# Thirty-two-byte gaps between the weight blocks of a fused attention and feed-forward kernel

## The chip, the core and the metric

The kernel runs on one core of a Trainium2 chip. The time is device microseconds of one execution, and the figure for a kernel is the median of several executions. Before the change the median of 3 runs is 677.4 us (677.21 to 677.68).

## The reference

Sliding-window attention with a few sink positions feeds a two-layer network whose first layer is followed by a leaky rectifier with one slope per hidden unit. All is float32.

```python
batch, n_heads, seq, head_dim = (4, 8, 768, 64); n_sink, window = (4, 128)
n_tokens, d_model, d_ff = (3072, 512, 2048)

scores = q @ k.T / 8;  keep = (pos_k < n_sink) | ((rel >= 0) & (rel < window))
a = exp(scores - max) / (sum + 1e-9);  attn = a @ v          # masked scores are -1e9
x = attn laid out as (3072, 512)
h = x @ w_in
g = maximum(h, 0) + alpha * minimum(h, 0)
return g @ w_out
```

## The kernel before

**Tiling.** The 3072 tokens are handled in 12 chunks of 256. In each chunk the attention of 8 heads is worked out, and its result stands in SBUF, transposed, as two tiles of four 128x256 blocks: `xh`, the value rounded to TensorE's fast float32 form, and `xl`, the rest. The hidden width of 2048 is cut into 16 blocks of 128, `f` = 0 to 15. A block's two weight matrices are in SBUF for the whole program in one tile `w0` to `w15` of 8192 bytes per partition: first `w_in`'s slice, high part and low part (2048 bytes each), then `w_out`'s slice, high and low part.

**The two products.** For each chunk and block, `gemm1` issues 12 matmuls (line 894): four steps along d_model, in each of them high weights by `xh`, high weights by `xl`, low weights by `xh`. The weights are the stationary operand (128 columns, 512 bytes per partition), `x` is the moving one (256 columns, 1024 bytes). The result is turned into `g` by lines 898 (ScalarE) and 899 (VectorE) and split into `gh` (line 900, ScalarE) and `gl` (line 901, VectorE). `gemm2` then issues 6 matmuls: here half of `gh` or `gl` is stationary (512 bytes) and a `w_out` slice moves (512 columns, 2048 bytes): lines 931 (high) and 932 (low) for each half of `gh`, and line 929 for each half of `gl`. Between a block's `gemm1` and its `gemm2` stand the products of the two blocks after it, and the attention of the next chunk is strewn between them. In all there are 12 x 16 x 12 = 2304 matmuls of the first and 12 x 16 x 6 = 1152 of the second kind, and each has a weight load of its own.

**The order.** A planner written in Python simulates the engines with a table of costs and fixes the order of all instructions on every engine while the program is built. It knows nothing of where in SBUF a tile lies. Around the place that the prediction reads, TensorE's order is (bank, moving or stationary tiles, shape):

```order
L894 MATMUL bank5_69<-xh1_116,w15_1207 128x256
L931 MATMUL bank6_70<-w13_1071,gh2_123 128x512
L932 MATMUL bank6_70<-w13_1071,gh2_123 128x512
L931 MATMUL bank7_71<-w13_1071,gh2_123 128x512
L932 MATMUL bank7_71<-w13_1071,gh2_123 128x512
L929 MATMUL bank6_70<-w13_1071,gl2_126 128x512
L929 MATMUL bank7_71<-w13_1071,gl2_126 128x512
L894 MATMUL bank4_68<-xh0_115,w0_305 128x256
...
L931 MATMUL bank6_70<-w14_1148,gh0_121 128x512
L932 MATMUL bank6_70<-w14_1148,gh0_121 128x512
```

So the second product of block 13 is followed by the first product of block 0 of the next chunk, and that by the second product of block 14.

**Where tiles lie.** Tiles are taken from pools. The pool `const` comes first in SBUF, and its tiles lie one behind the other in the order in which they are first asked for; each starts at a multiple of 32 bytes. A weight block's place is first asked for where its raw values are loaded (`load_weights`, line 371), the raw 64-bit values and the finished block share the tag `w{f}` and so the place. The places of blocks 13, 14 and 15 are first lent to tiles of the beginning (`lend`, lines 414 to 430). Behind `const` stands the pool `main` with `kq`, `pt_`, `comb`, `x`, `g` and the others.

Of the kernel before, what the change touches and what calls it, by code (L numbers as in the profile page):

```python
# [9 lines left out]
F32 = mybir.dt.float32  # L10
# [9 lines left out]
P = 128  # L20
# [58 lines left out]
class Plan:  # L79
# [20 lines left out]
    def held(self, tile_):  # L100
        v = Value(None)
        v.at = tile_
        return v

    def op(self, engine, cost, run, reads=(), writes=(), tail=0.09, mode=None, nbytes=0, other=None, locks=False):
        o = Op(engine, cost, tail, run, self.rank if engine == "PE" else None)
        o.ways = {engine: (cost, run)}
        if other:
            o.ways[other[0]] = other[1:]
        o.born = self.rank  # L110
        if engine == "PE":
            self.rank += 1
        o.mode, o.nbytes, o.index = mode, nbytes, len(self.ops)
        seen = []
        for group, writing in ((reads, False), (writes, True)):
            for x in group:
                v, key = x if isinstance(x, tuple) else (x, None)
                if v not in seen:
                    seen.append(v)
                keys = [k for k in set(v.wrote) | set(v.read) if key is None or k is None or k == key]  # L120
                for k in keys:
                    o.before.update(v.wrote.get(k, ()))
                    if writing:
                        o.before.update(v.read.get(k, ()))
                if writing:
                    for k in keys:
                        if key is None or k == key:
                            v.wrote.pop(k, None)
                            v.read.pop(k, None)
                    v.wrote.setdefault(key, []).append(o)  # L130
                else:
                    v.read.setdefault(key, []).append(o)
        for v in seen:
            v.left += 1
        o.values = seen
        o.takes = [v for v in seen if v.kind]
        o.locks = locks
        self.ops.append(o)
        return o
# [182 lines left out]
def program(ctx, tc, qk, pairs, vp, vq, vs, w, par, out):  # L322
    nc = tc.nc
    const = ctx.enter_context(tc.tile_pool(name="const", bufs=1))
# [42 lines left out]
    def load_weights(f, engine="ACT"):  # L367
        raw = raws[f] = held(None)

        def run():  # L370
            raw.at = const.tile([P, 2 * DM, 2], I32, tag=f"w{f}", name="wraw")
            (nc.sync if engine == "SP" else nc.scalar).dma_start(
                raw.at.rearrange("p (i x) w -> p i (x w)", i=2), w[f].bitcast(I32).rearrange("i p x -> p i x"))
        return op(engine, ISSUE if engine == "SP" else 0.12, run, writes=[raw] + lent.get(f, []), nbytes=8 * P * 2 * DM)
# [35 lines left out]
    lent = {}  # L410

    def lend(f, shape, count):
        box = {}

        def part(i):
            if "tile" not in box:
                box["tile"] = const.tile([P, count, *shape], F32, tag=f"w{f}", name="lent")
            return box["tile"][:, i]
        out_ = []
        for i in range(count):  # L420
            v = held(None)
            v.bind, v.box = lambda i=i: part(i), box
            out_.append(v)
        lent[f] = out_
        return out_

    early = lend(NF - 1, [QC + KC], 3) + lend(NF - 2, [QC + KC], 1)
    shared = const.tile([P, 1, QC + KC + 4 * WIN], F32, tag=f"w{NF - 2}", name="lent")
    early[3].box["tile"] = shared[:, :, :QC + KC]
    early_v = lend(NF - 3, [3, 2, D], 4)  # L430

    def bound(v):
# [845 lines left out]
```

## Time and profile before

| | before |
|---|---|
| median of 3 runs | 677.4 us |
| profiled execution, first to last instruction | 676.2 us |
| TensorE (PE) busy | 663.8 us, 98% of the span |
| weight loads (PEld) busy | 580.5 us, 86% |
| VectorE (DVE) busy | 525.8 us, 78% |
| ScalarE (ACT) busy | 397.5 us, 59% |
| granted TensorE clock, mean | 0.994 |

The span is the time from the first to the last instruction of one profiled execution; 1.2 us of the median lie around it. Matmuls are pipelined: a record's length runs from its start to the modelled end of its last column, and the next one starts long before that. What a matmul takes of TensorE's time is therefore read from the distance between the starts of two of them, not from the length of one.

### The profile page before, as it was taken

Reading aid. Unit: us, or ns where it says so; the run is one execution under the profiler, and the core shown is the slowest. Engines: PE = TensorE matmul, PEld = TensorE weight load, DVE = VectorE, ACT = ScalarE, POOL = GpSimd, SP = SyncE. Lnnn points to the kernel's source line nnn. Section 1 sums busy time; section 2 is a strip of 40 time slices with the busy share of each in tenths; the row PEclk is TensorE's granted clock in tenths of the full one; section 3 lists DMA queues with packets and bytes.
Section 4 is the critical chain, followed back from the end, with each engine's and each line's share of the span. In section 5 each row is a group of like instructions: output and inputs, shape, how many; then the busy total and the mean of one; then the engine's idle time right before and its main releaser. Section 6 shows DMA issues by size and latency. Waiting matters only on the chain.

```text
span 676.2 us, 13243 instructions
## 1 busy us (share of the span) xinstructions
PE 663.8 (98%) x4532; PEld 580.5 (86%) x4534; DVE 525.8 (78%) x1750; ACT 397.5 (59%) x1066; POOL 34.5 (5%) x115
## 2 busy tenths in 40 slices
PE   9989999999999999999999999999999999999996
PEld 4577898888989989989988988988998988998995
DVE  6999999968967976986986995995895994994331
ACT  6989888827636726736636735644744753853332
POOL 2110000001000000000000000010000000000000
PEclk9979999999999999999999999999999999999999
DMA  8684641424343453443443433552542543420001
GB/s 314 229 277 151 241 187 39 127 71 147 122 133 107 122 148 93 145 132 95 141 118 114 143 107 93 163 140 61 172 128 78 161 128 88 142 94 17 32 2 35
DMA packets 58683, 85.19 MB, mean 126 GB/s; under 512 B 9072, under 2 KB 35056, under 8 KB 58608
## 3 DMA queue, kind: packets, MB, share of 16 engines
q1 hardware_dynamic: 55056, 71.17, 34.7%
q10 hardware_dynamic: 3552, 13.11, 5.4%
q8 instruction: 37, 0.61, 0.4%
q14 instruction: 38, 0.31, 0.1%
HBM read 67.22 MB, written 17.04 MB: 125 GB/s over the span
## 4 chain that ended last, share of the span: by engine, by line
PE 83%; DVE 9%; ACT 5%; issue 2%; POOL 0%; DMA 0%; ACTq 0%; SPq 0%; POOLq 0%
PE bank L894 35%; PE bank L931 12%; PE bank L932 11%; PE bank L929 11%; PE bank L786 3%; PE bank L598 3%; PE bank L597 3%; PE bank L875 2%; DVE wa L396 2%; ACT pt L614 1%; ACT wa L382 1%; DVE wa L394 1%; DVE w L404 1%; DVE g L899 1%; DVE gl L901 1%
## 5 line engine op out<-in xcount | busy, mean ns | idle before, releaser
L894 PE MATMUL bank<-xh,w 128*128 128x256 f32 x1536 | 307.9, 283 | 0.4 <-DVE g L899 0.2
L894 PEld LDWEIGHTS bank<-xh,w 128*128 128x128 f32 x1536 | 250.6, 189 | 9.0 <-DVE g L899 3.0
L894 PE MATMUL bank<-xl,w 128*128 128x256 f32 x768 | 215.1, 280 | 0.1
L898 ACT ACTIVATE g<-bank,param 128x256 f32<-128x256 f32 x192 | 90.5, 472 | 117.4 <-PE bank L894 113.1
L931 PE MATMUL bank<-w,gh 128*128 128x512 f32 x382 | 151.7, 397 | 0.2 <-ACT gh L900 0.2
L932 PE MATMUL bank<-w,gh 128*128 128x512 f32 x382 | 150.1, 393 | 0.0
L894 PEld LDWEIGHTS bank<-xl,w 128*128 128x128 f32 x768 | 145.2, 189 | 4.4 <-DVE xl L808 0.3
L614 ACT ACTIVATE pt<-pt,nm 128x260 f32<-128x260 f32 (+1 forms) x192 | 94.5, 493 | 53.5 <-DVE nm L610 53.1
L899 DVE TENSOR_TENSOR g<-bank,g 128x256 f32<-128x256 f32 x192 | 79.7, 419 | 51.4 <-ACT g L898 50.9
L929 PE MATMUL bank<-w,gl 128*128 128x512 f32 x382 | 119.5, 394 | 0.0
L900 ACT CAST gh<-g 128x256 fp32r<-128x256 f32 x192 | 76.9, 404 | 59.7 <-DVE g L899 59.6
L901 DVE TENSOR_TENSOR gl<-g,gh 128x256 fp32r<-128x256 f32 x192 | 80.5, 423 | 26.5 <-ACT gh L900 23.0
L610 DVE CUSTOM_DVE_ANT_0 pt<-bank,masks 128x260 f32<-128x260 f32 (+1 forms) x192 | 75.0, 401 | 19.3 <-PE bank L598 15.5
L929 PEld LDWEIGHTS bank<-w,gl 128*128 128x128 f32 x382 | 70.7, 188 | 16.2 <-issue 0.7
L931 PEld LDWEIGHTS bank<-w,gh 128*128 128x128 f32 x382 | 71.9, 188 | 9.5 <-ACT gh L900 0.7
L932 PEld LDWEIGHTS bank<-w,gh 128*128 128x128 f32 x382 | 71.9, 188 | 8.3
L563 DVE TENSOR_TENSOR kq<-stage,kq 64x392 fp32r<-64x392 f32 x80 | 45.3, 566 | 2.7
L659 POOL TENSOR_TENSOR sink<-pt,ri 128x8 f32<-128x8 f32 x80 | 20.8, 264 | 504.7 <-DVE ri L644 358.8
L597 PE MATMUL bank<-kq 128*128 128x260 f32 (+1 forms) x160 | 44.4, 278 | 1.3 <-DVE nm L610 1.3
L598 PE MATMUL bank<-kq 128*128 128x260 f32 (+1 forms) x160 | 45.0, 281 | 0.0
L655 DVE CUSTOM_DVE_ANT_0 comb<-pt,ri 128x128 f32<-128x128 f32 x136 | 43.1, 343 | 0.4
L561 ACT CAST kq<-stage 128x392 fp32r<-128x392 f32 x80 | 40.9, 512 | 0.7 <-ACT pt L614 0.2
(130 smaller groups left out, 686.9 us busy)
## 6 DMA issues: line engine op xcount, KB each, us to landing
stage<-qk SPq DMA_DIRECT2D x80, 324.0 KB, 2.9
wraw<-w ACTq DMA_DIRECT2D x12, 1024.0 KB, 5.9
swap<-comb SPq DMA_DIRECT2D x36, 256.0 KB, 2.0
comb<-swap SPq DMA_DIRECT2D x36, 256.0 KB, 3.2
v<-vq SPq DMA_DIRECT2D x36, 192.0 KB, 2.5
out_dram<-ob SPq DMA_DIRECT2D x22, 256.0 KB, 3.5
wraw<-w SPq DMA_DIRECT2D x4, 1024.0 KB, 12.0
v<-vp SPq DMA_DIRECT2D x8, 192.0 KB, 6.9
```

Of the source, the lines that this page charges most:

```text
L597: nc.tensor.matmul(s[:, w0], qh()[:, qs], ks()[:, kw], start=True, stop=False)
L598: nc.tensor.matmul(s[:, w0], ql()[:, qs], ks()[:, kw], start=False, stop=True)
L610: op("DVE", dve(n), lambda: nc.vector.tensor_tensor_reduce(out=pt.at[:, u, w0], in0=s.at[:, w0], in1=masks[:, i, w0], scale=-0.125, scalar ...
L614: op("ACT", exp(n), lambda: nc.scalar.activation(pt.at[:, u, w0], pt.at[:, u, w0], AF.Exp, bias=nm.at[:, h, u:u + 1], scale=-1.0, accum_ou ...
L894: nc.tensor.matmul(h(), fin.at[:, 0, part, ks], rhs.at[:, kt], start=(kt == 0 and n == 0), stop=(kt == KT - 1 and n == 2))
L898: op("ACT", act(QC, True), lambda: nc.scalar.activation(g.at, h(), AF.Copy, scale=alt[:, f:f + 1]), reads=[bk, known("param")], writes=[g])
L899: op("DVE", dve(QC), lambda: nc.vector.tensor_tensor(g.at, h(), g.at, ALU.max), reads=[bk], writes=[g])
L900: op("ACT", cast(QC), lambda: nc.scalar.copy(gh.at, g.at), reads=[g], writes=[gh])
L901: op("DVE", dve(QC), lambda: nc.vector.tensor_tensor(gl.at, g.at, gh.at.bitcast(F32), ALU.subtract), reads=[g, gh], writes=[gl])
L929: nc.tensor.matmul(o2[j].at, gl.at[:, js], fin.at[:, 1, 0], start=False, stop=(f == NF - 1))
L931: nc.tensor.matmul(o2[j].at, gh.at[:, js], fin.at[:, 1, 0], start=(f == 0), stop=False)
L932: nc.tensor.matmul(o2[j].at, gh.at[:, js], fin.at[:, 1, 1], start=False, stop=False)
```

## The change

A tile of 8 floats (32 bytes per partition) is asked for ahead of each weight block whose place isn't lent, and one more behind the place that block 14 shares with the tiles of the beginning. Nothing reads or writes these tiles. No operation, no operand's shape, no order and no semaphore is another: on every engine the instructions stand in the same order as before, with the same waits.

```diff
@@ load_weights
         def run():
+            if f not in lent:
+                const.tile([P, 8], F32, name=f"gap{f}")
             raw.at = const.tile([P, 2 * DM, 2], I32, tag=f"w{f}", name="wraw")
@@ after lend(...)
     early[3].box["tile"] = shared[:, :, :QC + KC]
+    const.tile([P, 8], F32, name="gap")
     early_v = lend(NF - 3, [3, 2, D], 4)
```

What is another is where tiles start. In bytes modulo 512, by the program's own table of tiles:

| tile | before | after |
|---|---|---|
| w14 | 192 | 192 |
| w15 | 32 | 64 |
| w0, w13 | 32 | 96 |
| w1, w2, w3, ... w12 | 32 | 128, 160, 192, ... 480 (32 more each time) |
| xh, xl, g, gh, gl, sinkT, vs, ob (all) | 224 | 160 |
| comb, wa (all) | 256 | 192 |
| kq0, kq1 | 96, 128 | 32, 64 |
| ident | 320 | 352 |

A weight slice is 512 or a multiple of 512 bytes away from its block's start, and so is each part of `xh`, `xl`, `gh` and `gl`. So one number modulo 512 says where the two operands of all matmuls of a block lie to each other. For `gemm1` (place of `x` less place of the block) it was 192 for 15 blocks and 32 for block 14. It is now 64 for blocks 0 and 13, 32, 0, -32, -64, ... -320 for blocks 1 to 12 (-320 is 192 again), -32 for block 14 and 96 for block 15. For `gemm2` it is the same number with the other sign. Within the pool `main` all tiles are moved by the same 448 bytes.

## The prediction

> **What bounds the kernel now.** I looked first at the busy time by stretch, since no instruction is added or moved and only an engine that sets the end can pass a change on. Columns: stretch; its length; busy time and instructions of TensorE, of weight loads, VectorE, ScalarE and GpSimd; granted clock, DMA share, GB/s.
>
> ```profile
> 0.00:20.00 20.00, 18.34 (x98) 8.87 (x99) 13.47 (x61) 13.09 (x36) 4.40 (x22) 1.00 0.90 327
> 20.00:60.00 40.00, 37.13 (x235) 27.33 (x235) 38.16 (x86) 36.89 (x93) 5.24 (x10) 0.91 0.62 216
> 100.00:150.00 50.00, 49.42 (x333) 43.46 (x332) 44.81 (x149) 33.55 (x89) 2.72 (x8) 1.00 0.27 78
> 200.00:300.00 100.00, 100.00 (x689) 90.55 (x687) 82.31 (x303) 57.38 (x165) 5.28 (x17) 1.00 0.41 120
> 300.00:400.00 100.00, 100.00 (x699) 89.84 (x699) 79.54 (x293) 57.46 (x166) 3.99 (x16) 1.00 0.42 123
> 400.00:500.00 100.00, 100.00 (x711) 90.20 (x710) 78.75 (x285) 57.19 (x165) 5.36 (x17) 1.00 0.42 122
> ```
>
> From 200 us on TensorE never stops, at the full clock; before that it stops for 1 to 7% of a stretch. The other engines have room. So nearly every nanosecond that a matmul's start-to-start distance gains or loses goes into the time. Most of these matmuls are of the two products; the groups (busy time, mean length of one, idle time before) are:
>
> ```profile
> L894 PE MATMUL bank<-xh,w 128*128 128x256 f32 x1536 | 307.9, 283 | 0.4 <-DVE g L899 0.2
> L931 PE MATMUL bank<-w,gh 128*128 128x512 f32 x382 | 151.7, 397 | 0.2 <-ACT gh L900 0.2
> L932 PE MATMUL bank<-w,gh 128*128 128x512 f32 x382 | 150.1, 393 | 0.0
> L894 PE MATMUL bank<-xl,w 128*128 128x256 f32 x768 | 215.1, 280 | 0.1
> L929 PE MATMUL bank<-w,gl 128*128 128x512 f32 x382 | 119.5, 394 | 0.0
> ```
>
> They wait for almost nothing (0.2 us and less). What is left is how fast one matmul follows the other, and here the timeline has something odd. Four pieces of it follow, of TensorE alone (start, length, line, tiles): block 9's first product in one chunk and in the next, the second product of block 13, and that of block 14.
>
> ```profile
> 336.98 0.28 PE L894 MATMUL bank<-xl,w 128*128 128x256 f32 x1
> ...
> 338.28 0.28 PE L597 MATMUL bank<-kq 128*128 128x260 f32 x1
> ...
> 388.76 0.28 PE L894 MATMUL bank<-xl,w 128*128 128x256 f32 x1
> ...
> 390.01 0.28 PE L597 MATMUL bank<-kq 128*128 128x260 f32 x1
> 390.24 0.40 PE L931 MATMUL bank<-w,gh 128*128 128x512 f32 x1
> ...
> 391.64 0.28 PE L894 MATMUL bank<-xh,w 128*128 128x256 f32 x1
> ...
> 411.46 0.39 PE L931 MATMUL bank<-w,gh 128*128 128x512 f32 x1
> ...
> 412.83 0.28 PE L894 MATMUL bank<-xh,w 128*128 128x256 f32 x1
> ...
> 414.22 0.40 PE L931 MATMUL bank<-w,gh 128*128 128x512 f32 x1
> ...
> 415.63 0.28 PE L597 MATMUL bank<-kq 128*128 128x260 f32 x1
> ```
>
> Block 9: eleven matmuls in 1.30 us at the first place (118 ns each) and in 1.25 us at the second (114 ns). Same weights, same relative place, same clock, no waits; two speeds. A sequence of matmuls mostly keeps one speed from its second or third member to its last. So place alone does not decide: something in the timing does too, and the place can at most say which speeds there are. Second products: six matmuls take 1.40 us for block 7 (from 390.24), 1.37 us for block 13 and 1.41 us for block 14, thus 233, 228 and 235 ns each. Block 14 is the only one that lies elsewhere relative to `x` and `g` (32 instead of 192). Read over all chunks by the distances between starts (waits left out), the first product has a mean of 116.2 ns, from 114.4 (block 2) to 117.6 (block 11), and block 14 has 117.2; the second has 231.0 ns over the other 15 blocks, from 229.4 to 232.3, and block 14 has 234.2, the slowest of the 16.
>
> What runs beside a matmul is the load of the next one's weights (here from 414.22 on, with the weight loads shown):
>
> ```profile
> 414.23 0.19 PEld L932 LDWEIGHTS bank<-w,gh 128*128 128x128 f32 x1
> 414.46 0.40 PE L932 MATMUL bank<-w,gh 128*128 128x512 f32 x1
> 414.46 0.19 PEld L931 LDWEIGHTS bank<-w,gh 128*128 128x128 f32 x1
> ```
>
> Each load starts within some 10 ns of the matmul that it lies under, so the two reads of SBUF march side by side from a fixed offset. I looked for VectorE and ScalarE work beside fast and slow matmuls and found no instruction whose presence separates them by more than 2 ns of 116; so I take the pair of reads on TensorE itself as the place where an address can act. That this is the cause is argued, not shown.
>
> **The change part by part.** The gap tiles cost no instruction, so nothing is removed, added or moved in any queue: 0 us. The 448 bytes by which the pool behind is moved change no distance within it: the scores' and values' matmuls meet their operands as before. What changes is the distance between `x` or `g` and the weights, for 14 of 16 blocks: all but block 12, which gets 192 again, and block 14, which goes from 32 to -32, one odd place for another. Those 14 blocks, 12 chunks, are 168 units of 12 + 6 matmuls.
>
> The trace has no row for most of the new places; it has bounds.
> - From below: every matmul at the fast speed that the trace shows, 113.3 ns and 226.7 ns (block 9 at 388.76 is nearly there; 113 or 114 and 226 are the commonest distances among quick matmuls). 168 x (12 x 2.9 + 6 x 4.3) = 168 x 60.6 ns = 10.2 us less, 667.2 us.
> - The other place that the trace has, block 14's: 168 x (12 x 1.0 + 6 x 3.2) = 168 x 31.2 ns = 5.2 us more, 682.6 us.
> - From above: the slowest steady distances in block 14's second product, 0.24 us (414.22 to 414.46), for all its kind, and 118 ns for the first: 168 x (12 x 1.8 + 6 x 9) = 168 x 75.6 ns = 12.7 us more, 690.1 us.
>
> Of the value between I take half of block 14's price. For it: of two places seen, the odd one is the slower, and the few matmuls under which a load from another pair of tiles runs (the last `kq` matmul before a product), which meet at other offsets, are no quicker than the mean. Against the full price: the first product shows only 1.0 ns, well inside the spread of blocks that share one place (114.4 to 117.6), and sixteen places must hold better ones than 32 too. 677.4 + 2.6 = 680.0 us. The sum is made as a difference, so it stands against the median; against the profiled execution it is 676.2 + 2.6 = 678.8 us of span.
>
> The cover: before 200 us part of a slower matmul would hide in TensorE's own stops (7% of 20 to 60 us, about 1% of 100 to 150 us); that trims the sum by under 0.2 us and I leave it. A slower TensorE makes nobody else late; a faster one would at most meet VectorE, which is busy 79 to 82% there. The DMA share is 0.90 in the first 20 us: if other start addresses made each transfer 5% longer, that is 1 us at the most, and from 100 us on (0.27 to 0.42) nothing.
>
> [...]
>
> **The rivals.**
> 1. *No effect.* The speed is a matter of timing alone and the distance modulo 512 means nothing, or only something finer than 32 bytes counts, which all these gaps leave as it was. For it: 15 blocks at one place differ among themselves by 3.2 ns, about as much as block 14 from their mean. Against it: block 14's second product repeats its slow distances in chunk after chunk. Block 14's own surplus stays; 677.4 us, within 676.1 to 678.7.
> 2. *Faster: 192 is a bad place.* At 192 moving and weight reads meet in about half of the matmuls; at most other places they pass each other, and a product that has fallen into the quick speed keeps it. For it: a quick stretch stays quick to its end, and a single spread cannot hold all blocks at one bad place. Half of what lies between the mean and the fast speed: 5.1 us less, 672.3 us; the floor is 667.2. This decides once more than about half of the 14 blocks fall below 115 ns in their first product.
> 3. *Slower in full*, as block 14 or worse: 682.6 us, up to 690. I count it with my forecast's side.
>
> **How the numbers follow.** About 0.2% (1.35 us) is what a measurement of this kernel can tell from no change. Slower by more than that, the forecast with rival 3: 0.42, with a range of its own from 678.8 to 687. No effect, and small sums of either sign: 0.25. Faster: 0.33. The range must take in rival 2's value and some of the way to its floor, and rival 3's value with some of what lies above: 670 to 687 us leaves about one in ten out on either side, a little less above.
>
> **What would show it.** Right: the order and waits of all engines as before; per-block distances that now differ by block in a steady way over the chunks, with blocks 1 to 11 on the mean 0.5 ns (first product) and 1.6 ns (second) above 116.2 and 231.0; block 1, which now lies at 32, slow as block 14 was (234 in the second product); block 12, at 192 again, unchanged. Wrong: block means that are a copy of the old ones (rival 1), or many blocks whose first product takes no more than 1.37 us for twelve matmuls throughout (rival 2). A shift of TensorE's stops before 200 us by more than 1 us would say that something other than the distances moved.

## Result: slower by 0.6%, and the profile after

The changed kernel takes 681.5 us (median of 5 runs, 680.53 to 684.65) against 677.7 us (median of 5 runs of the kernel before in the same comparison). The ratio is 1.0058, 95% interval 1.0038 to 1.0078: some 3.9 us more.

The stretches of the profile after, with the columns of the prediction's first fence:

```profile
20.00:60.00 40.00, 36.42 (x247) 26.22 (x249) 39.24 (x88) 38.57 (x96) 5.39 (x10) 1.00 0.59 216
200.00:300.00 100.00, 100.00 (x684) 90.29 (x684) 82.42 (x302) 57.10 (x164) 5.28 (x17) 1.00 0.41 120
300.00:400.00 100.00, 100.00 (x695) 89.96 (x692) 78.91 (x290) 57.57 (x166) 3.99 (x16) 1.00 0.41 122
400.00:500.00 100.00, 100.00 (x707) 90.16 (x706) 78.29 (x282) 56.96 (x165) 5.14 (x17) 1.00 0.41 122
```

From 200 to 500 us TensorE is still busy without a pause, at the same clock, and gets through fewer matmuls in the same time: 684, 695 and 707 where it was 689, 699 and 711. From 20 to 60 us it does more than before (247 against 235), at a granted clock of 1.00 in this execution against 0.91 in the one profiled before, and it reaches the 500th matmul of the program's own 1.6 us earlier (90.0 us before, 88.4 us after); so the two profiled spans differ by only 2.4 us (676.2 and 678.6). From that matmul to the last one it is 580.2 us before and 584.2 us after.

The groups:

```profile
L897 PE MATMUL bank<-xh,w 128*128 128x256 f32 x1536 | 310.3, 283 | 0.3
L897 PE MATMUL bank<-xl,w 128*128 128x256 f32 x768 | 215.8, 281 | 0.1
L934 PE MATMUL bank<-w,gh 128*128 128x512 f32 x382 | 151.6, 397 | 0.0
L935 PE MATMUL bank<-w,gh 128*128 128x512 f32 x382 | 150.8, 395 | 0.0
L932 PE MATMUL bank<-w,gl 128*128 128x512 f32 x382 | 120.3, 396 | 0.0
```

No wait has been added. The modelled lengths hardly show what happened; the distances between starts do. Two pieces of TensorE's timeline after, the first products of block 8 and of block 10 in one chunk:

```profile
385.79 0.28 PE L897 MATMUL bank<-xl,w 128*128 128x256 f32 x1
...
387.05 0.28 PE L600 MATMUL bank<-kq 128*128 128x260 f32 x1
...
392.08 0.28 PE L897 MATMUL bank<-xl,w 128*128 128x256 f32 x1
...
393.39 0.40 PE L934 MATMUL bank<-w,gh 128*128 128x512 f32 x1
```

Block 8 now lies at 320: eleven matmuls in 1.26 us, 114.5 ns each. Block 10 lies at 256: eleven in 1.31 us, 119 ns each, more than either speed that was seen at its place before the change (114 and 118 ns). Over all chunks, by the distances between starts with waits left out, the first product went from 116.2 to 117.9 ns and the second from 231.2 to 232.5 ns. 2304 x 1.65 + 1152 x 1.27 ns = 5.3 us; the measured 3.9 us are less. Part of it falls where TensorE stops anyway: from the 500th matmul on, the distances without a wait add up to 4.7 us more, and those with a wait to 0.6 us less.

By block, the mean of the first product (place of `x` less place of the block, in brackets): 119.5 (256), 119.6 (96), 119.2 (352), 119.1 (0), 118.6 (384), 118.4 and 118.1 (480), 118.2 (224), 117.9 (416), 117.7 and 117.1 (64), 117.5 (32), 117.3 (288), 116.3 (320), 116.1 (192) and 115.5 (448). So the speed seems to go with the place, and 192, which the blocks had by chance, is one of the three best. This list alone doesn't prove it, since before the change blocks at one place differed by 3.2 ns; the runs below do.

### The profile page after: what moved, and what is told of

Read it like the earlier page. It is cut to its first block, busy times and chain, and to the rows that moved or that the text cites. A ratio compares the mean times of both kernels' runs of the same rounds, so it can differ in the third digit from the quotient of the medians.

```text
span 678.6 us, 13245 instructions
## 1 busy us (share of the span) xinstructions
PE 666.3 (98%) x4534; PEld 582.1 (86%) x4534; DVE 526.4 (78%) x1750; ACT 398.2 (59%) x1066; POOL 34.5 (5%) x115
## 4 chain that ended last, share of the span: by engine, by line
PE 89%; DVE 5%; ACT 4%; issue 1%; DMA 0%; POOL 0%; ACTq 0%; SPq 0%; POOLq 0%
PE bank L897 39%; PE bank L934 13%; PE bank L935 13%; PE bank L932 13%; PE bank L789 3%; PE bank L601 3%; PE bank L600 3%; PE bank L878 2%; ACT pt L617 1%; DVE wa L398 1%; ACT wa L384 1%; PE bank L862 1%; DVE pt L613 1%; DVE w L406 1%; ACT w L403 0%
```

## The experiments

Two theories stood at first: A, the distance between the moving operand and the weights sets the speed of the pair of reads; B, the harm comes from a distance that changes from block to block, which throws TensorE out of step. A third, C, was that any move of the tiles reshuffles the speeds.

### One common distance of 256, of 448, and a move by 512

The kernel before, with nothing but one tile ahead of the pool that holds `x` and `g`, of 64, 256 or 512 bytes:

```diff
+    pool.tile([P, 16], F32, name="shift")      # 16 floats; 64 in the second run, 128 in the third
     several("stage", 2, [P, QC + KC], F32)
```

> No gaps; instead one tile of 64 bytes ahead of the pool that holds x and g, so that all blocks but 14 lie at one common distance to x again, 256 instead of 192 (block 14 at 96). Theory A, the distance itself sets the speed: in the kernel with the gaps the block that lay at 256 (block 10) had a first product of 119.5 ns a matmul against 116.2 before, and a second one of 231.0, as before. All blocks at 256: first product near 119.5, 2304 x 3.3 ns = 7.5 us more, about 685 us. Theory B, the harm is the spread, a distance that differs from block to block: with one common distance the time is that of before, 677 us, and the first product 116.2 ns.

> As the run at 256, with a tile of 256 bytes: all blocks but 14 at the distance 448 (block 14 at 288). Theory A: the block that lay at 448 with the gaps (block 4) had 115.5 ns in the first product and 231.5 in the second, so 0.7 ns x 2304 less and 0.3 ns x 1152 more: 1.3 us less than before, about 676 us; no change or a little faster. Theory B: 677 us. A loss of 3 us or more would speak against both.

> A tile of 512 bytes ahead of the pool of x and g: every tile of that pool moves by 512 bytes, all distances modulo 512 are those of before. Theory A: 677 us, first product 116.2 ns, the block means within about 1 ns of before. Theory C, the speed goes by absolute places or any move of the tiles reshuffles it: another time by some us, block means that are not those of before.

| common distance | time (before: 677.4) | ratio, 95% | first product | second product |
|---|---|---|---|---|
| 256 | 683.7 us | 1.0090 (1.0070 to 1.0110) | 119.4 ns | 231.3 ns |
| 448 | 677.6 us | 1.0002 (0.9991 to 1.0012) | 116.2 ns | 231.2 ns |
| 192, all moved by 512 | 677.2 us | 0.9990 (0.9980 to 1.0000) | 116.3 ns | 231.3 ns |

The stretches at the common distance of 256, and then those at 448:

```profile
200.00:300.00 100.00, 100.00 (x679) 90.65 (x678) 81.55 (x299) 57.68 (x165) 5.49 (x17) 1.00 0.40 120
300.00:400.00 100.00, 100.00 (x693) 90.03 (x692) 78.50 (x289) 57.12 (x165) 3.98 (x16) 1.00 0.39 120
```

```profile
200.00:300.00 100.00, 100.00 (x687) 90.45 (x686) 82.32 (x302) 57.38 (x165) 5.29 (x17) 1.00 0.41 121
300.00:400.00 100.00, 100.00 (x701) 89.93 (x700) 79.54 (x293) 57.47 (x166) 3.97 (x16) 1.00 0.40 123
```

At 256 every block is slow, 119.0 to 119.7 ns, and the kernel loses more than with the gaps, without any distance that changes from block to block. So B falls as the cause. C falls with the other two: 14 of their 16 block means of the first product are within 0.5 ns of those of before (blocks 0 to 3 at 448: 115.8, 115.5, 114.4, 117.0; before: 115.8, 115.5, 114.4, 117.0), and only blocks 12 and 13 differ by 1.0 to 1.5 ns. That 448 gives the picture of 192, not the 115.5 that block 4 had there with the gaps, was not expected: at these two places, 256 bytes apart, the first product has one speed, 116.2 ns. The prediction's "modulo 512" was too wide. And where the distance modulo 256 is the same and the places are not, the speed is nearly the same: with the gaps block 2 and `x` both lay at 160 modulo 256 and the first product took 119.1 ns, here the blocks and `x` both lie at 32 and it takes 119.4.

### Gaps of 256 bytes

```diff
+            if f in (1, 4, 7, 10):
+                const.tile([P, 64], F32, name=f"gap{f}")
             raw.at = const.tile([P, 2 * DM, 2], I32, tag=f"w{f}", name="wraw")
```

> Gaps again, but of 256 bytes and ahead of blocks 1, 4, 7 and 10 alone: the blocks lie at five different distances from x by absolute bytes, all equal modulo 256. Theory A: 677.4 us, and block by block the means of before (first product 115.8, 115.5, 114.4, 117.0 ns for blocks 0 to 3). If gaps between blocks as such, or a distance that changes from block to block, do the harm: slower, towards 681 us.

677.2 us, ratio 0.9995 (0.9981 to 1.0009); first product 116.2 and second 231.2 ns, blocks 0 to 3 at 115.8, 115.5, 114.4 and 117.0. So in this kernel neither gaps as such nor distances that differ by a multiple of 256 change anything that these numbers show.

### x alone, g alone

```diff
+    pool.tile([P, 16], F32, name="shift")      # x alone
     several("xh", 2, [P, KT, QC], F32R)
     several("xl", 2, [P, KT, QC], F32R)
+    pool.tile([P, 48], F32, name="back")       # x alone; g alone has 16 floats here and none above
     several("g", 2, [P, QC], F32)
```

> Only x is moved: 64 bytes ahead of xh, 192 more ahead of g, so that x lies at 0 modulo 256 from the blocks (it was at 192), while g and all else keep their places modulo 256. Theory A (distance between the moving operand and the next weights, modulo 256): the whole loss of the run at 256 comes back, as its first product went to 119.4 ns and its second stayed at 231.3: first product 119.4 here, second 231.2, about 6.3 us more, 683.7 us. If the loss came from g, or from anything else that was moved there: 677.4 us.

> Only g, gh and gl are moved, by 64 bytes (w_out then lies at 0 from them modulo 256, it was at 64); x stays at 192. Theory A with the run at 256: first product 116.2, second 231.3 ns, no change, 677.4 us. If the place of g mattered as x's does: some 3 ns on 1152 matmuls, 3.5 us more.

`x` alone: 683.3 us, ratio 1.0089 (1.0071 to 1.0107), first product 119.4 and second 231.0 ns. That is the whole loss of the run at 256, so it came from `x` and the blocks. `g` alone: 677.5 us, ratio 1.0003 (0.9993 to 1.0013). The time was as expected, the way to it was not: the second product became quicker, 229.3 ns (231.2), and the first slower, 116.7 ns (116.2), though its own operands lay as before. It is slower not only at its edge, where it meets `g`, but by 0.5 to 0.9 ns from its sixth matmul to its eleventh. So in this run the first product changed with the place of the second product's operands, which aren't its own. The two means would make 1.3 us less together; with the waits, the trace from the 500th matmul on has 1.7 us less in the second product, 1.1 us more in the first and 0.2 us more in the matmuls of `kq`. The 0.5 us that remain are within the interval of the time.

### TensorE alone, at 32 places

The next runs leave the whole computation out; TensorE works on constant tiles and, but for the last run, nothing else runs beside it. There is one execution of each. The first has the pattern of the first product at each place, 36 matmuls, up and then down, and 18 matmuls of 512 columns likewise (`steps` goes from 0 to 496 bytes, then back; the last `...` stands for the rest of the call):

```diff
+        for s in steps:
+            for r in range(3):
+                for kt in range(4):
+                    ks = slice(kt * P, (kt + 1) * P)
+                    for part, n in ((0, 0), (0, 1), (1, 0)):
+                        nc.tensor.matmul(h[:, :256], w[:, part * 512 + kt * P:part * 512 + (kt + 1) * P],
+                                         x[:, s + kt * 256 + n * 512:s + kt * 256 + n * 512 + 256] if kt < 2 else x[:, s + (kt - 2) * 256 + n * 512:s + (kt - 2) * 256 + n * 512 + 256],
...
```

> Leaves the whole computation out: TensorE alone issues the first product's pattern of 36 matmuls (256 columns, each with its weight load) at 32 distances between moving operand and weights, 0 to 496 bytes in steps of 16, up and down again, and 18 matmuls of 512 columns at each. Nothing else runs. Theory A: the distance between starts differs with the place in steady steps of some ns (113 to 120 for 256 columns), the same on the way up and down; places 64, 192, 320 and 448 are among the quickest, 0, 96, 256 and 352 among the slowest. If other engines or the timing alone are the cause: one distance between starts at all places.

Equal stretches of 3 us on the way up at 96, 112, 192 and 256 bytes; the count behind PE busy is what to read (it takes in the two or so matmuls that began before the stretch):

```profile
36.50:39.50 3.00, 3.00 (x27) 3.00 (x26) 0.00 (x0) 0.00 (x0) 0.00 (x0) 1.00 0.00 0
40.70:43.70 3.00, 3.00 (x29) 3.00 (x28) 0.00 (x0) 0.00 (x0) 0.00 (x0) 1.00 0.00 0
61.90:64.90 3.00, 3.00 (x29) 3.00 (x29) 0.00 (x0) 0.00 (x0) 0.00 (x0) 1.00 0.02 5
79.00:82.00 3.00, 3.00 (x27) 3.00 (x27) 0.00 (x0) 0.00 (x0) 0.00 (x0) 1.00 0.02 5
```

With VectorE, ScalarE and GpSimd idle, the same matmul takes 113.3 ns at 112 and 192 and 119.8 to 120.0 at 96 and 256. The second half of the scan repeats the first 256 bytes on: 96 and 352 both 120.0, 64 and 320 both 117.8, 16 and 272 both 118.6 on the way up. At 22 of the 32 places the steady speeds up and down are within 1 ns. Some have two: 144 had 118.7 on the way up and 113.3 on the way down, 448 had 113.3 and then 117.8. And a change of place can take time to settle: at 112, coming from above, eleven distances of 116 to 121 ns went by before the steady 113. The expected list of quick and slow places was half right: 192 and 448 were quick, 64 and 320 were not (117.8).

### The kernel's alternation at 256 pairs of places, and at steps of 4 bytes

A unit is now what the kernel does for a block, 12 matmuls of 256 and 6 of 512 columns, three times at each pair of places of `x` and `g`.

> Leaves the whole computation out: TensorE alone issues the kernel's own alternation, 12 matmuls of the first product and 6 of the second, three times at each of 256 pairs of places (x at 0 to 240 bytes from the weights modulo 256, g likewise, steps of 16). The bare run before it showed the speed repeating with 256 bytes and needing up to ten matmuls to settle at a new place, so a unit of 12 and 6 should not be the sum of the two steady speeds. Theory A: units differ by place, from 2.72 us (12 x 113.3 + 6 x 226.7 ns) to about 2.84 us (12 x 120 + 6 x 234), and the kernel's place (x at 192, g at 192) lies in the lower half, near the 2.78 us (12 x 116.2 + 6 x 231.2) of the kernel before. If timing alone rules: all pairs alike, or a scatter that does not go with the place.

Units differ by place, about as theory A had it. The mean unit was 2808 ns, the shortest 2747 and the longest 2846; at `x` and `g` both at 192 it took 2751 to 2760. The place of `x` matters about twice as much as that of `g`: averaged over the other, units go from 2781 to 2824 ns by `x` and from 2795 to 2816 ns by `g`. The first product's means by place of `x`, beside the means of the kernel's blocks at that place modulo 256 (the gapped kernel; 0 also from the run at 256):

| place of x | 0 | 32 | 64 | 96 | 128 | 160 | 192 | 224 |
|---|---|---|---|---|---|---|---|---|
| TensorE alone, ns | 119.0 | 117.1 | 117.3 | 119.5 | 119.2 | 118.7 | 116.1 | 118.2 |
| blocks of the kernel, ns | 119.1, 119.5 (run at 256: 119.4) | 117.5, 117.3 | 117.7, 117.1, 116.3 | 119.6, 119.2 | 118.6 | 117.9 | 116.1, 115.5 | 118.2, 118.4, 118.1 |

A program in which nothing but TensorE runs gives the kernel's block means within 1 ns, the order of the places nearly throughout. So the effect comes without the work of any other engine, and the cause is sought in what TensorE does alone, its matmuls and the weight loads beside them.

> The alternation of 12 and 6 matmuls with nothing else running, as the run with pairs, now with x at all 64 places from 0 to 252 bytes in steps of 4 and g at 192, 208, 240 and 0. The run with pairs had 2781 ns a unit at the place 192 (mean over g), the next best 2797 (32) and the worst 2824 (96). If the reads meet in lines or banks of 16 or 32 bytes, the four places within 16 bytes are alike (within 10 ns), and 192 to 204 stand below all others. If it is counted in single elements, neighbours at 4 bytes differ by as much as those at 16, and a place below 2750 ns may stand between.

Neither reading was right as it stood. Places at 0 or 12 bytes past a multiple of 16 took 2802 and 2797 ns a unit, those at 4 and 8 bytes 2837 and 2824: on the mean the four places within 16 bytes are thus not alike. No group of places stood out: the shortest mean was 2787 ns, at 28. And the kernel's own pair, 2751 to 2760 ns in the run before, now took 2807, and in the last run 2760 again: one pair of places, two speeds. The pairs that ran before it were others.

### What is the partner?

> Leaves the whole computation out: TensorE alone issues the first product's pattern at 16 places (0 to 240 bytes, steps of 16), once with weight loads of 128 columns and once with loads of 32 columns, the moving operand unchanged. If the partner of the moving read is the weight load: with 32 columns the place matters a quarter as much or not at all, all places within 1 to 2 ns of 113.3. If the moving read alone meets something at certain places: the same 113 to 120 ns by place with both.

```diff
-    for times, steps in ((0, STEPS), (1, STEPS[::-1])):
+    for cols in (P, 32):
         ...
-                        nc.tensor.matmul(h[:, :256], w[:, part * 512 + kt * P:part * 512 + (kt + 1) * P], ...
+                        nc.tensor.matmul(h[:cols, :256], w[:, part * 512 + kt * P:part * 512 + kt * P + cols], ...
```

```profile
L30 PE MATMUL h<-x,w 128*128 128x256 f32 x576 | 70.0, 285 | 8.5 <-ACT x L24 8.5
L30 PEld LDWEIGHTS h<-x,w 128*128 128x128 f32 x576 | 69.8, 193 | 8.5 <-ACT x L24 8.5
L30 PE MATMUL h<-x,w 128*32 128x256 f32 x576 | 66.5, 277 | 0.0
L30 PEld LDWEIGHTS h<-x,w 128*32 128x32 f32 x576 | 62.2, 108 | 4.2
```

The loads went from a mean of 193 to 108 ns, and the matmuls under which they run, though their moving operand has the same columns at the same places, became quicker at most places. With 128 columns 2 of the 16 places run at 113.3 ns and the others at 116.7 to 120.0 (the first place left out); with 32 columns 9 of 16 are at 113.3 and the others at 116.4 to 117.7. So the place of the moving operand alone does not set the speed. The shorter matmul also writes 32 instead of 128 rows of its result, so this run alone can't tell the load from that; but in the gapped kernel it was the place of the weights that differed from block to block (first product 115.5 to 119.6 ns), and in the trace the weight load is the instruction that has them as its input. That the load is the partner is inferred from the two together; no run shows it by itself. The effect did not come down to a quarter, nor to 1 to 2 ns everywhere; seven places keep 3 to 4 ns.

### Other engines beside TensorE

> Leaves the whole computation out: the alternation of 12 and 6 matmuls at one place, the kernel's own (x and g at 192), 120 units in four stretches. In the first TensorE is alone; in the first half of the second and of the fourth VectorE adds two tiles in SBUF without a pause, in most of the third ScalarE copies one. Two speeds were seen at this one place in the kernel (114 and 118 ns). If other engines' reads and writes of SBUF throw TensorE from one speed into the other: one speed while it is alone, and another, or a change of speed, where VectorE or ScalarE sets in. If the speed hangs on how TensorE came to the place: no change at these points.

The instructions fell out otherwise than planned: VectorE's and ScalarE's work both ran beside the first stretch, and from about 91 us on, but for the very end, TensorE was alone.

```profile
20.00:80.00 60.00, 60.00 (x393) 54.63 (x392) 55.43 (x132) 55.67 (x138) 0.00 (x0) 1.00 0.00 1
140.00:200.00 60.00, 60.00 (x394) 54.73 (x393) 0.00 (x0) 0.00 (x0) 0.00 (x0) 1.00 0.00 1
220.00:280.00 60.00, 60.00 (x394) 54.69 (x394) 0.00 (x0) 0.00 (x0) 0.00 (x0) 1.00 0.00 1
```

With both engines at over 55 of 60 us and with both idle, TensorE does the same; each unit after the first took 2760 ns, also where the other engines' work ended. At this place these adds and copies in SBUF didn't throw TensorE from one speed into the other. Reads of PSUM (where the matmuls' results stand), GpSimd's work and heavy DMA beside it were not tried.

What goes with block 9's 118 and 114 ns stands in the profile before, just ahead of the two pieces that the prediction showed:

```profile
336.65 0.22 PE L597 MATMUL bank<-kq 128*128 128x132 f32 x1
...
388.41 0.28 PE L597 MATMUL bank<-kq 128*128 128x260 f32 x1
```

In chunks 2 to 10 (counted from 0), the two `kq` matmuls that stand just ahead of block 9's first product have 132 columns three times, and then it runs at 118 ns, and 260 columns six times, and then at 114 ns. The runs at 448, moved by 512 and with gaps of 256 have the same in all nine chunks. So here too the speed goes with what TensorE does just before; a run that changes only that was not made.

No version came out that beats both kernels. In the run with pairs the place of the kernel before is the best of the 16 for `x` (2781 ns a unit, the next 2797), and moving `g` gained nothing in the time (677.5 us); of the other places for `x`, only 0 (the run at 256) was tried in the kernel as a common one.

## Why the prediction was right, point by point

- **What bounds the kernel**: right. From 200 to 650 us TensorE is busy for 449.8 of 450 us before and 449.9 after, and from the 500th matmul on the two products are 4.1 us longer, waits included, and all the rest 0.2 us shorter.
- **The pair of reads as the place of action**: right in that TensorE alone is enough: in the bare runs the speed goes by place (113.3 to 120.0 ns) while no other engine works, and with shorter weight loads 9 of 16 places run at 113.3 ns where 2 did. That it is the two reads that act on each other was argued there and isn't shown. Right too is its caution that the place says only which speeds there are: with a common distance of 192 block 9 has 114 or 118 ns by what stands ahead of it, at 256 all blocks have 119 to 120 ns in all chunks. That block's two pieces were not alike in all but the speed, as the prediction had it: the `kq` matmuls ahead of them differ (132 and 260 columns).
- **Modulo 512**: too wide. At 192 and 448, 256 bytes apart, the first product has 116.2 ns, and the place within 16 bytes counts too (2797 to 2837 ns a unit on the mean). Counted modulo 256, block 4 (448) was at 192 again, as block 12 was, block 8 (320) lay where blocks 0 and 13 lie (64), and 13 blocks left the place 192, not 14.
- **The price**: 2.6 us were forecast, some 3.9 us came. The step that failed is the taking of half of block 14's price for both products. The first product was given 0.5 ns (1.0 us in 14 blocks) and lost 1.65 (3.8 us in all 16); the second was given 1.6 ns (1.6 us) and lost 1.3 (1.5 us). The cover was given under 0.2 us, and from the 500th matmul on waits hid 0.6 us; the one error made up for a part of the other. Block 14's place, 32, is one of the milder places for the first product (117.5 where others have 119.6), and its 234 ns in the second product weren't a matter of that place alone: block 1, which took over the place, has 232.5. That the sign came out is in part luck: one odd place in the trace said "slower" by a ns or three, the forecast gave it 0.42, and that the old place is among the best no row of the trace could tell.
- **Block 12 unchanged**: 116.1 and 231.0 ns, against 117.5 and 231.6 before; right within the 1.0 to 1.5 ns by which this block also moved in the runs at 448 and by 512.
- **No effect (rival 1)**: fell. The kernel became some 3.9 us slower, and with all else idle the same matmul takes 113.3 to 120.0 ns by place.
- **192 a bad place (rival 2)**: fell; of the 16 places in the run with pairs it is the best. What stands from it is that a quick stretch mostly stays quick: in the profile before, a distance of at most 114 ns within a first product is followed by another such one in 612 of 627 cases (products with nothing between their matmuls).
- **DMA and the first 60 us**: no loss there: the DMA share of the first 20 us is 0.90 before and after, and the profiled execution was even ahead by 1.6 us at the 500th matmul, at a granted clock of 1.00 against 0.91. TensorE's stops before 200 us add up to 6.6 us before and 6.5 us after, so the sign that something other than the distances moved did not come.

## What to carry to other kernels

In this kernel TensorE is busy throughout and each float32 matmul has its own weight load. There the distance from the weight tile to the moving tile, modulo 256 bytes, was worth up to 6% of a matmul of 256 columns (113.3 against 120.0 ns, TensorE alone) and 0.9% of the kernel's time (683.7 against 677.4 us). Look at the distance between starts by weight block, since busy time (98% of the span before and after) and waits showed nothing of it. A scan over places costs one run in which TensorE alone repeats the kernel's pattern, and its means carried over to this kernel within about 1 ns. Before spreading tiles over all places, see which place they have: here the spread gave 117.9 ns in the first product, with blocks from 115.5 to 119.6, and the one place that they had shared, with 116.2, was among the best.

## What the runs showed that was not expected

- Places 256 bytes apart ran alike: with moves by 256 and 512 bytes and with gaps of 256 the first product has 116.2 or 116.3 ns, as before.
- The moving operand's start within 16 bytes counts: in the run at steps of 4 bytes, 4 or 8 bytes past a multiple of 16 cost 22 to 40 ns in a unit of 2800 against 0 or 12 bytes past it.
- One pair of places had two steady speeds, about 2760 ns a unit in two runs and 2807 in a third, in which other pairs of places came before it. In the kernel block 9 has 118 ns behind `kq` matmuls of 132 columns and 114 ns behind those of 260; by which step one leads to the one speed and the other to the other stays open.
